# Sliding-window attention with an MLP behind it: a third buffer for natural keys and queries, fillers in each cycle of the opening, and the later mask built in the middle

## The chip, the core and the metric

The kernel runs on one core of one Trainium2 chip. The core has five engines that run side by side and wait for each other through semaphores: TensorE (matmul, PE in the profile), VectorE (DVE), ScalarE (ACT), GpSimd (POOL) and SyncE (SP). SyncE and GpSimd issue the transfers between the main memory and the on-chip memory (SBUF); matmuls write into a small accumulator memory (PSUM). Each engine takes its instructions strictly in the order in which the program gives them. The metric is the device time of the whole program in microseconds (us); lower is better. The profile also shows the clock that TensorE was granted, as a share of its full speed.

## The reference

There are 8 batches of 8 heads over 576 positions with 64 elements per head. Each position sees the positions at most 32 away, and 8 global positions see and are seen by all. The result is reordered to 4608 tokens of 512 features and goes through an MLP with a 2048 wide hidden layer and the activation `h * cos(h)`.

```python
mask = np.abs(pos[:, None] - pos[None, :]) <= 32
mask = mask | is_global[:, None] | is_global[None, :]
scores = np.where(mask, scale * np.matmul(q, k.transpose(0, 1, 3, 2)), -1e9)
attn = softmax(scores)
x = np.matmul(attn, v).transpose(0, 2, 1, 3).reshape(4608, 512)
h = x @ w_in
out = (h * np.cos(h)) @ w_out
```

## The kernel before, in words

**Units of work.** Two heads form a pair; there are 32 pairs, four to a batch, and two pairs (four heads) form a half, numbered s. For a pair the program forms scores in blocks of keys (`scores`, L673), takes the exponential on ScalarE, multiplies with a 0/1 mask on VectorE (this gives `pm`), multiplies with the values into the accumulator `pv` (`values`, L694), scales by the reciprocal of the sums (`xn`, VectorE), and turns the result into `xT` (`turn_x`, L718), which is the MLP's input with features on partitions.

**Two ways of loading.** The first four halves (pairs 0 to 7, `HY` = 4) take their keys and queries in natural order: `load_qk` (L271) lets GpSimd's queue bring the keys and the queries of a half, cast to fp16, into `kn` and `qn`, of which there are two buffers each, used in turn. `local_k` and `local_q` (L580, L591) turn them on TensorE, and ScalarE copies them out; pairs 0 to 3 also pick their global rows there (`pick_globals`). Their values come in fp32 through SyncE's queue (`load_vn`, five transfers, L368; `load_vn_rows`, the global rows, two transfers, L376) and are cast by GpSimd (`cast_vn`, L388). These pairs use five blocks and the mask `mask5` (`scores5`, `values5`, `turn_x5`). All later pairs use eleven blocks and the mask `mask` and come through casts into fp16 copies in the main memory (`cast_half`, L259, GpSimd's queue) and transposing transfers from there (`turn_half`, L278, SyncE's queue). The global rows of k, q and v are fetched by `gather` (L328, indirect transfers on GpSimd's queue).

**Later mask.** `build_mask` (L411) forms `mask` on VectorE in two parts. The first part needs two index tables that GpSimd writes (L955, L956); the second part ends with L437, L439 and L441.

**Order.** The schedule is written by hand. Behind some setup, the list `FRONT` (L57) orders the opening, in which pairs 0 to 7 run; each word is a step: `s`, `p` and `x` with a pair's number are its scores, its values and the turn of its result; `k` and `q` its local keys and queries; `L` loads keys and queries of a half, `W` a quarter of w_in (`load_w_in`), `O` w_out; `C` casts a half's values; `Y` runs `late_iotas` (a gather and the two index tables); `Z0` and `Z1` are the two parts of the later mask, `Z2` clears; `H0` casts the gathered rows and `H1` turns them; `g` copies the global columns of a pair; `c` and `K` cast the v and the k and q of a half into the main memory; `B` starts the turns and value loads of a half; `m` is one group of first-layer matmuls and `t` its activation; `+` and `-` allow or forbid the use of spare accumulators. `f` with a number issues so many fillers (`fill`, L471): matmuls of ones, 128 by 128 weights and 184 columns, into a part of `pv` that nothing reads. `MID` (L49) orders the work of s = 3, where `1` is a first-layer group with its activation and `2` a part of a second-layer sum; then follow the lists for the other halves, and at the end the rest of the MLP alone.

**w_out.** Its fp16 tile `w_out16` is allocated beside `w_in16`, is filled by step `O`, and is first read at s = 4.

Of the kernel before, what the change touches and what calls it, by code (L numbers as in the profile page):

```python
# [10 lines left out]
FP16 = mybir.dt.float16  # L11
# [6 lines left out]
B, H, S, D = 8, 8, 576, 64  # L18
NT, DM, DFF = 4608, 512, 2048
P = 128  # L20
NP = H // 2
QB = 56
NB = 11
G = 8
# [21 lines left out]

ORDER = "sa 2 2 2 2 sz pa 1 1 2 xa pz G 1 1 2 xz n 1 1 2 kc qc 1 kd qd 2 1"

MID = "+ 1 1 1 1 Z1 K5 1 1 1 1 A0 n0 Z2 1 1 A1 1 1 kc qc n1 1 1 kd qd V K6 1 1 A2 n2 - B5 1 1"  # L49

FOURTH = ORDER

# [1 line left out]

SIXTH = "sa 2 2 2 2 sz pa 1 1 2 xa pz G 1 1 2 xz n 1 1 D0 2 kc qc D1 1 kd qd D2 2 1"

FRONT = ("s0 k1 q1 L2 Y0 w4 y0 s1 p0 k2 q2 Z0 f4 x0 p1 s2 W0 C1 H0 k3 q3 L3 f4 x1 H1 p2 s3 g4 g5 k4 q4 W1 C2 x2 p3 "  # L57
         "s4 g6 g7 k5 q5 x3 C3 c4 K4 p4 s5 k6 q6 W2 x4 p5 s6 k7 q7 W3 O x5 p6 s7 B4 m m x6 p7 t t + m m t t x7 -")
WARM = 13
OK_ALL = float(P * (B * NP * 2 * BP + B))  # L60

# [143 lines left out]
def kernel(  # L205
# [41 lines left out]
    xT = keep.tile([P, NC, NT + 40], FP16)  # L247

    NV = 4
    kT = [keep.tile([P, 2, KT], FP16, name=f"kT{i}") for i in range(2)]  # L250
    qT = [keep.tile([P, 2, QT], FP16, name=f"qT{i}") for i in range(2)]
    kn = [keep.tile([KP, 2 * 2, RW, D], FP16, name=f"kn{i}") for i in range(2)]
    qn = [keep.tile([QP, 2 * 2, RW, D], FP16, name=f"qn{i}") for i in range(2)]
    vw = [keep.tile([P, NB, 2, D + 1], FP16, name=f"vw{i}") for i in range(NV)]
    NK = 4
    kw = [keep.tile([P, NB, P], FP16, name=f"kw{i}") for i in range(NK)]
# [14 lines left out]
    def load_qk(s, hs=(0, 4)):  # L271

        base = (s * 4 + hs[0]) * S * D
        for src, dst in ((k, kn[s % 2][KPAD : KPAD + S // RW]), (q, qn[s % 2][0 : S // RW])):
            nc.gpsimd.dma_start(dst[:, hs[0] : hs[1]].rearrange("x h r d -> x h (r d)"),
                                dview(src, base, (RW * D, S // RW), (S * D, hs[1] - hs[0]), (1, RW * D)))

# [25 lines left out]
    def pick_globals(pr, t, src, ones, n, to):  # L303

        h0 = 2 * (pr % 2)
        for r in range(RW):
            for h in range(2):
                nc.tensor.matmul(t[h * D : (h + 1) * D], src[:n, h0 + h, r], ones[:n, r], start=r == 0, stop=r == RW - 1, skip_group_check=True)
        nc.scalar.copy(to, view(t, (0, to.shape[1]), (1, G)))
# [18 lines left out]
    def gather(src, dst, half):  # L328
        rows = src.rearrange("b h s d -> (b h s) d")
        for h in range(2):  # L330
            nc.gpsimd.indirect_dma_start(
                out=dst[:, half, h], out_offset=None, in_=rows,
                in_offset=bass.IndirectOffsetOnAxis(ap=gidx_rows[:, 0:1], axis=0),
                element_offset=(half * 32 + h) * S * D)
# [46 lines left out]
    def hold(pr):  # L381

        nc.gpsimd.tensor_copy(gate, qb[pr % NK][0:1, 0, G : G + 1])
# [155 lines left out]


    w_in16 = const.tile([P, NC, DFF], FP16)
    w_out16 = const.tile([P, NF, DM], FP16)

    r_all = keep.tile([P, B * NP, 2 * BP], FP32)
    x_sq = keep.tile([P, B * NP // 2], FP32)
# [24 lines left out]
    def turned(src, pr, n):  # L570

        bank = ps.tile([P, 512], FP32, tag="h", bufs=2, name="bank")
        t = view(bank.bitcast(FP16), (QP, RW), (1, QP))
        h0 = 2 * (pr % 2)
        for r in range(RW):
            for h in range(2):
                nc.tensor.transpose(t[h * D : (h + 1) * D, r, 0:n], src[:n, h0 + h, r], ident16[:n, :n])
        return t, bank[:, 400 : 400 + G]

    def local_k(pr):  # L580
        to = kw[pr % NK][:, :, G:]
        if pr < 2 * HY:
            t, g = turned(kn[pr // 2 % 2], pr, KP)
            if pr < HY:
                pick_globals(pr, g, kn[pr // 2 % 2], one_k, KP, k5(pr)[:, :, 0:G])
            nc.scalar.copy(k5(pr)[:, :, G:].rearrange("p n (j r) -> p n j r", r=RW),
                           view(t, (KS // RW, NK5), (1, KS // RW), (QP, RW)))
        else:
            nc.vector.tensor_copy(to, view(kT[pr // 2 % 2][:, pr % 2], (QB, NB), (1, W)))  # L589

    def local_q(pr):  # L591
        to = qb[pr % NK][:, :, G:]
        if pr < 2 * HY:
            t, g = turned(qn[pr // 2 % 2], pr, QP)
            if pr < HY:
                pick_globals(pr, g, qn[pr // 2 % 2], one_q, QP, q5(pr)[:, 1:, 0:G])
            nc.scalar.copy(qb[pr % NK][:, 0, 0:G], t[:, :, 0])
            nc.scalar.copy(q5(pr)[:, :, G:].rearrange("p n (j r) -> p n j r", r=RW),
                           view(t[:, :, 1:], (KS // RW, NK5), (1, KS // RW), (QP, RW)))
        else:  # L600
            nc.vector.tensor_copy(to, view(qT[pr // 2 % 2][:, pr % 2], (QB, NB), (1, QB)))
# [21 lines left out]
    def values5(pr):  # L623
        pm, vp, h0 = pm_of.pop(pr), vn16(pr // 2), 2 * (pr % 2)
        X = D + 1

        def add(h, t, c0, m, slot, p0, start, stop):
            nc.tensor.matmul(pv[p0 : p0 + m, h, X * slot : X * slot + X], pm[:, h * CN + OFF[t] + c0 : h * CN + OFF[t] + c0 + m], vp[:, t, h0 + h],  # L628
                             start=start, stop=stop, skip_group_check=True)

        for group in ((0, 1, 4), (2, 3)):
            for t in group:
                for h in range(2):
                    add(h, t, D if t else 0, P if t < 4 else WID[4] - D, t, 0, t == 0, False)
            for t in group:
                for h in range(2):
                    if t:
                        add(h, t, 0, D, t - 1, D, False, t == 3)
                    else:
                        add(h, 0, P, G, 1, 0, False, False)  # L640
        den = pv[:, :, D : D + 1]
        rp = r_all[:, pr]
        dg = work.tile([G, 2], FP32, tag="dg")
        nc.vector.tensor_reduce(dg, view(pv[0:G, :, X + D : X + D + 1], (512, 2), (X, 4)), AX.X, ALU.add)
        nc.vector.reciprocal(view(rp, (NK5, 2), (1, NK5)), view(den, (512, 2), (X, NK5)))
        nc.vector.reciprocal(view(rp[0:G, 1:], (NK5, 2), (1, 4)), view(dg, (1, 2), (0, 4)))
        if pr % 2 == 0:
            xn_of[pr // 2] = work.tile([P, 2, BP, P], FP16, tag="xn", bufs=4, name="xn")
        xn = xn_of[pr // 2][:, pr % 2]
        nc.vector.tensor_tensor(  # L650
            view(xn, (D, 2), (P, NK5), (1, D)), view(pv, (512, 2), (X, NK5), (1, D)),
            view(rp, (NK5, 2), (1, NK5), (0, D)), ALU.mult)
# [209 lines left out]
    with tc.manual_schedule():  # L862
# [2 lines left out]
        nc.vector.memset(ones16, 1.0)  # L865
        nc.vector.memset(pio2, pi / 2.0)
        nc.vector.memset(kn[0][0:KPAD, 0:2], 0.0)
        for t in (qn[0][64:QP, 2:4], kn[0][0:KPAD, 2:4], qn[1][64:QP], kn[1][0:KPAD]):
            nc.scalar.memzero(t.rearrange("p a b c -> p (a b c)"))
        load_qk(0, (0, 2))  # L870
        nc.gpsimd.iota(p_i, pattern=[[0, 1]], base=0, channel_multiplier=1)
# [12 lines left out]
        build_band()  # L884
        index_rows(1)
        load_vn(0)
        gather(v, vg32, 0)
        load_qk(1)
        build_ones()
        build_mask5()  # L890
        local_k(0)
# [2 lines left out]
        warm(4)  # L894
        for s in range(1, HY):
            nc.vector.memset(vn_of(s)[0 : 64 if s == 1 else 32, 0], 0.0)
        for s in range(1, HY):
            load_vn(s)
            load_vn_rows(s)
        for i in range(NV):  # L900
            nc.vector.memset(vw[i][:, :, :, D : D + 1], 1.0)
            if i % 2:
                nc.vector.memset(vw[i][:, NB - 1, :, 0:D], 0.0)
        cast_vn(0)
        gather(k, kg32, 0)
        pv = ps.tile([P, 2, 512], FP32, tag="pv", bufs=1)
        nc.vector.memset(pv, 0.0)
        nc.vector.memset(view(pv[:, :, D : D + 1], (512, 2), (65, 6)), 1.0)
# [40 lines left out]
            load_values(2 * s)  # L949
            load_values(2 * s + 1)  # L950

        def late_iotas(_):

            gather(q, qg32, 0)
            nc.gpsimd.iota(kid_i, pattern=[[QB, NB]], base=-(G + 32), channel_multiplier=1)  # L955
            nc.gpsimd.iota(d_i, pattern=[[-1, C]], base=0, channel_multiplier=1)  # L956

        LOCAL = {"k": local_k, "q": local_q}
        OTHER = LOCAL | {"g": globals_kq, "L": load_qk, "W": load_w_in, "c": lambda s: cast_half(s, "v"), "v": load_values, "n": x_squares,
                 "C": cast_vn, "w": warm, "y": value_rows, "Y": late_iotas, "V": lambda _: hold(9), "H": early_globals, "Z": steady_buffers, "f": fill, "r": load_vn, "A": later_rows, "D": later_globals, "O": load_w_out, "K": lambda s: cast_half(s, "kq" if s == 4 else "vkq"), "B": bring, "m": lambda _: one(False), "t": lambda _: mlp_act()}  # L960
        ready[0] = 1
        for step in FRONT.split():
            if step in "+-":
# [89 lines left out]
```

## Time and profile before

| what | value |
|---|---|
| time, median of 3 runs | 367.63 us (366.43 to 369.79) |
| the profiled execution's own time | 364.79 us |
| its span, first to last instruction | 362.9 us |
| mean granted clock of TensorE | 0.949 |
| TensorE, matmuls busy | 339.1 us (93%) |
| VectorE busy | 253.4 us (70%) |
| ScalarE busy | 239.3 us (66%) |
| GpSimd busy | 107.3 us (30%) |
| moved by DMA | 45.69 MB, mean 126 GB/s |

The times of the rows of a timeline are the start, in us from the span's beginning, and the length; then come the engine, the line of the program, the operation, the tiles written and read, their shapes, and how many; in brackets stands how long the engine stood before it and what let it go. `q0` is the DMA queue that GpSimd fills, `q1` the one that SyncE fills. A row by stretches has its bounds and its length, then busy time and instructions of an engine, and behind them the granted clock, the DMA engines' busy share and GB/s.

### The profile page before, as it was taken

Reading aid. Unit: us, or ns where it says so; the run is one execution under the profiler, and the core shown is the slowest. Engines: PE = TensorE matmul, PEld = TensorE weight load, DVE = VectorE, ACT = ScalarE, POOL = GpSimd, SP = SyncE. Lnnn points to the kernel's source line nnn. Section 1 sums busy time; section 2 is a strip of 40 time slices with the busy share of each in tenths; the row PEclk is TensorE's granted clock in tenths of the full one; section 3 lists DMA queues with packets and bytes.
Section 4 is the critical chain, followed back from the end, with each engine's and each line's share of the span. In section 5 each row is a group of like instructions: output and inputs, shape, how many; then the busy total and the mean of one; then the engine's idle time right before and its main releaser. Section 6 shows DMA issues by size and latency. Waiting matters only on the chain.

```text
span 362.9 us, 8183 instructions
## 1 busy us (share of the span) xinstructions
PE 339.1 (93%) x3076; PEld 172.0 (47%) x3076; DVE 253.4 (70%) x600; ACT 239.3 (66%) x408; POOL 107.3 (30%) x218
## 2 busy tenths in 40 slices
PE   7787999688989899999999999999999999999992
PEld 3566764244444444445444445454444444444440
DVE  6758769877798768787877879686878355446310
ACT  6744686595767686868777787777877855644300
POOL 6567544652516404250605070402002000000000
PEclk9956559899999999999999999999999999999998
DMA  5999599999999999999999999999910001100111
GB/s 91 185 168 185 86 140 176 200 166 136 154 198 148 203 184 137 188 131 206 120 200 116 186 129 174 134 178 161 105 49 12 31 29 48 41 29 30 60 58 66
DMA packets 175559, 45.69 MB, mean 126 GB/s; under 512 B 163881, under 2 KB 170521, under 8 KB 175321
## 3 DMA queue, kind: packets, MB, share of 16 engines
q1 hardware_dynamic: 111657, 27.53, 54.1%
q0 software_dynamic: 63856, 17.57, 49.8%
q8 instruction: 26, 0.43, 0.5%
q14 instruction: 20, 0.16, 0.2%
HBM read 45.07 MB, written 20.05 MB: 179 GB/s over the span
## 4 chain that ended last, share of the span: by engine, by line
PE 75%; DVE 7%; DMA 6%; ACT 5%; issue 3%; SPq 3%; POOL 0%; ACTq 0%
PE po L763 32%; PE ph L746 30%; PE tx L728 2%; PE pv L628 2%; PE st L683 2%; DMA vn<-in_v_dram 2%; PE pv L703 2%; ACT e L686 2%; DMA vw<-vg 2%; DMA gidx_col<-in_global_idx_dram 1%; ACT e L691 1%; ACT cos L752 1%; PE pn L795 1%; DVE g L753 1%; SPq L402 1%
## 5 line engine op out<-in xcount | busy, mean ns | idle before, releaser
L746 PE MATMUL ph<-xT,w_in 128*128 128x512 f16 x576 | 144.3, 385 | 4.1 <-DVE g L753 2.9
L752 ACT ACTIVATE cos<-ph,pio 128x512 f16<-128x512 f32 x144 | 97.3, 687 | 68.9 <-PE ph L746 64.5
L763 PE MATMUL po<-w_out,g 128*128 128x512 f16 x576 | 139.4, 379 | 0.2 <-ACT o L768 0.2
L753 DVE TENSOR_TENSOR g<-cos,ph 128x512 f16<-128x512 f16 x144 | 96.1, 685 | 48.6 <-ACT cos L752 47.1
L746 PEld LDWEIGHTS <-w_in 128*128 128x128 f16 x576 | 54.6, 99 | 70.1 <-issue 12.7
L763 PEld LDWEIGHTS <-g 128*128 128x128 f16 x576 | 55.3, 98 | 65.5 <-issue 0.2
L937 POOL COPY gate<-xn 1x1 f16<-1x1 f16 x12 | 2.2, 181 | 132.3 <-DVE xn L714 132.3
L686 ACT ACTIVATE e<-st 128x512 f16<-128x512 f32 x48 | 26.0, 594 | 11.8 <-PE st L683 9.1
L687 DVE TENSOR_TENSOR pm<-e,mask 128x512 f16<-128x512 f16 x48 | 20.4, 426 | 19.1 <-ACT e L686 17.7
L268 POOL DMA_DIRECT2D q<-in_q_dram x12 | 26.1, 2175 | 0.0
L714 DVE TENSOR_TENSOR xn<-pv,r_all 128x768 f16<-128x768 f32 x24 | 23.0, 958 | 1.1
L781 ACT ACTIVATE xn<-xn 128x1536 f16<-128x1536 f16 (+1 forms) x16 | 22.8, 1422 | 0.0
L768 ACT COPY o<-po 128x512 f32<-128x512 f32 x18 | 10.6, 586 | 16.3 <-PE po L763 16.3
L268 POOL DMA_DIRECT2D k<-in_k_dram x12 | 19.8, 1652 | 0.2 <-issue 0.2
L770 DVE COPY o<-po 128x512 f32<-128x512 f32 x18 | 12.4, 690 | 8.8 <-PE po L763 8.2
L736 POOL COPY xT<-xg 128x4 f16 x48 | 15.4, 321 | 5.5 <-DVE xT L731 2.9
L616 ACT ACTIVATE e<-st 128x488 f16<-128x488 f32 x16 | 8.3, 572 | 13.0 <-PE st L613 13.0
L752 ACT ACT_TABLE_LOAD x13 | 16.7, 1283 | 0.2
L589 DVE COPY kw<-kT 128x1320 f16<-128x1320 f16 x24 | 16.3, 679 | 0.0
L628 PE MATMUL pv<-vw,pm 128*128 128x65 f16 (+3 forms) x160 | 13.4, 230 | 2.4 <-issue 1.1
L686 ACT ACT_TABLE_LOAD x12 | 15.4, 1283 | 0.2
L703 PE MATMUL pv<-vw,pm 128*64 128x65 f16 x528 | 14.0, 197 | 1.7 <-DMA vw<-vg 1.2
(173 smaller groups left out, 365.1 us busy)
## 6 DMA issues: line engine op xcount, KB each, us to landing
out_dram<-o SPq DMA_DIRECT2D x36, 256.0 KB
vw<-v SPq DMA_DIRECT2D x35, 165.0 KB
v<-in_v_dram POOLq DMA_DIRECT2D x12, 288.0 KB, 5.6
k<-in_k_dram POOLq DMA_DIRECT2D x12, 288.0 KB, 8.0
q<-in_q_dram POOLq DMA_DIRECT2D x12, 288.0 KB, 9.4
w_in<-in_moe_w_in_dram POOLq DMA_DIRECT2D x4, 512.0 KB
w_out<-in_moe_w_out_dram POOLq DMA_DIRECT2D x1, 2048.0 KB
vn<-in_v_dram SPq DMA_DIRECT2D x16, 120.0 KB
```

Of the source, the lines that this page charges most:

```text
L268: nc.gpsimd.dma_start(dst[s].rearrange("t (h d) -> t h d", h=4), dview(src, base, (D, S), (S * D, 4), (1, D)))
L589: nc.vector.tensor_copy(to, view(kT[pr // 2 % 2][:, pr % 2], (QB, NB), (1, W)))
L628: nc.tensor.matmul(pv[p0 : p0 + m, h, X * slot : X * slot + X], pm[:, h * CN + OFF[t] + c0 : h * CN + OFF[t] + c0 + m], vp[:, t, h0 + h], ...
L686: nc.scalar.activation(e[:, 0:512], st[h], AF.Exp, scale=scale)
L687: nc.vector.tensor_tensor(view(pm[:, h], (1, 512)), e[:, 0:512], view(mask, (1, 512)), ALU.mult)
L703: nc.tensor.matmul(pv[r0 : r0 + C, j // 6, c0 : c0 + 65], pm[:, h, j], vp[:, j, h], start=True, stop=True)
L714: nc.vector.tensor_tensor(view(xn, (384, 2), (D, 6), (1, D)), view(pv, (512, 2), (65, 6), (1, D)), view(rp, (6, 2), (1, 6), (0, D)), ALU.mult)
L746: nc.tensor.matmul(ph, w_in16[:, j, f * P : (f + 1) * P], xT[:, j, t * TT : (t + 1) * TT], start=(j == 0), stop=(j == NC - 1))
L752: nc.scalar.activation(cos, ph, AF.Sin, bias=pio2)
L753: nc.vector.tensor_tensor(g, cos, ph, ALU.mult)
L763: nc.tensor.matmul(po, g16[:, f, s * P : (s + 1) * P], w_out16[:, f], start=(f == 0), stop=(f == NF - 1))
L781: nc.scalar.activation(view(xn, (BP * P, 2), (1, n)), view(xn, (BP * P, 2), (1, n)), AF.Square, accum_out=x_sq[:, s : s + 1])
```

## The change

- `kn` and `qn` get a third buffer each, which lies in the room of `w_out16`; that tile is now allocated earlier. `load_qk` of half 2 is issued right behind that of half 1, and that of half 3 where half 2's stood. ScalarE clears the unused rows of the third buffers too.
- The two index tables are written before the first gather. The gather of k moves from the setup into step `Y`, where it stands together with that of q, behind the load of half 3.
- The values of half 2 are loaded before the global rows of half 1, and those of half 3 before the rows of half 2.
- `Z0` moves from `FRONT` to `MID`, where it stands right before `Z1`.
- `FRONT` has eight fillers before p0 and six before each of x0 to x5; before, it had four before x0 and four before x1. The steps `C`, `W`, `H`, `g` and `O` are placed anew.
- In `values5` all matmuls on whole blocks come first and those on the neighbours' parts behind them; before, blocks 0, 1 and 4 had both ahead of blocks 2 and 3.
- In `MID` one step `1` moves ahead of `A2`, and the spare accumulators are forbidden one place later.

```diff
-MID = "+ 1 1 1 1 Z1 K5 1 1 1 1 A0 n0 Z2 1 1 A1 1 1 kc qc n1 1 1 kd qd V K6 1 1 A2 n2 - B5 1 1"
+MID = "+ 1 1 1 1 Z0 Z1 K5 1 1 1 1 A0 n0 Z2 1 1 A1 1 1 kc qc n1 1 1 kd qd V K6 1 1 1 A2 n2 B5 - 1"
...
-FRONT = ("s0 k1 q1 L2 Y0 w4 y0 s1 p0 k2 q2 Z0 f4 x0 p1 s2 W0 C1 H0 k3 q3 L3 f4 x1 H1 p2 s3 g4 g5 k4 q4 W1 C2 x2 p3 "
-         "s4 g6 g7 k5 q5 x3 C3 c4 K4 p4 s5 k6 q6 W2 x4 p5 s6 k7 q7 W3 O x5 p6 s7 B4 m m x6 p7 t t + m m t t x7 -")
+FRONT = ("s0 k1 q1 L3 Y0 w4 y0 s1 f8 p0 k2 q2 f6 x0 p1 s2 C1 W0 k3 q3 f6 x1 p2 s3 H0 k4 q4 f6 x2 H1 g4 g5 C2 p3 "
+         "s4 W1 k5 q5 f6 x3 g6 g7 p4 s5 k6 q6 C3 c4 K4 f6 x4 p5 s6 k7 q7 W2 W3 O f6 x5 p6 s7 B4 m m x6 p7 t t + m m t t x7 -")
...
+    NN = 3
...
+    w_out16 = const.tile([P, NF, DM], FP16)
+    kn.append(w_out16[0:KP, 0:4].rearrange("p h (r d) -> p h r d", d=D))
+    qn.append(w_out16[0:QP, 4:8].rearrange("p h (r d) -> p h r d", d=D))
...
-        for src, dst in ((k, kn[s % 2][KPAD : KPAD + S // RW]), (q, qn[s % 2][0 : S // RW])):
+        for src, dst in ((k, kn[s % NN][KPAD : KPAD + S // RW]), (q, qn[s % NN][0 : S // RW])):
...
-        for group in ((0, 1, 4), (2, 3)):
-            for t in group:
-                for h in range(2):
-                    add(h, t, D if t else 0, P if t < 4 else WID[4] - D, t, 0, t == 0, False)
-            for t in group:
-                for h in range(2):
-                    if t:
-                        add(h, t, 0, D, t - 1, D, False, t == 3)
-                    else:
-                        add(h, 0, P, G, 1, 0, False, False)
+        for t in (0, 1, 4, 2, 3):
+            for h in range(2):
+                add(h, t, D if t else 0, P if t < 4 else WID[4] - D, t, 0, t == 0, False)
+        for t in (1, 4, 2, 3):
+            for h in range(2):
+                add(h, t, 0, D, t - 1, D, False, False)
+        for h in range(2):
+            add(h, 0, P, G, 1, 0, False, True)
...
-        for t in (qn[0][64:QP, 2:4], kn[0][0:KPAD, 2:4], qn[1][64:QP], kn[1][0:KPAD]):
+        for t in (qn[0][64:QP, 2:4], kn[0][0:KPAD, 2:4], qn[1][64:QP], kn[1][0:KPAD], qn[2][64:QP], kn[2][0:KPAD]):
...
         load_vn(0)
+        nc.gpsimd.iota(kid_i, pattern=[[QB, NB]], base=-(G + 32), channel_multiplier=1)
+        nc.gpsimd.iota(d_i, pattern=[[-1, C]], base=0, channel_multiplier=1)
         gather(v, vg32, 0)
         load_qk(1)
+        load_qk(2)
...
-        for s in range(1, HY):
-            load_vn(s)
-            load_vn_rows(s)
+        load_vn(1)
+        load_vn(2)
+        load_vn_rows(1)
+        load_vn(3)
+        load_vn_rows(2)
+        load_vn_rows(3)
...
         cast_vn(0)
-        gather(k, kg32, 0)
...
-        def late_iotas(_):
+        def late_gathers(_):
 
+            gather(k, kg32, 0)
             gather(q, qg32, 0)
-            nc.gpsimd.iota(kid_i, pattern=[[QB, NB]], base=-(G + 32), channel_multiplier=1)
-            nc.gpsimd.iota(d_i, pattern=[[-1, C]], base=0, channel_multiplier=1)
```

More of the change, by code (lines that the diff above doesn't have):

```diff
@@ L541 @@
     w_in16 = const.tile([P, NC, DFF], FP16)
-    w_out16 = const.tile([P, NF, DM], FP16)
     r_all = keep.tile([P, B * NP, 2 * BP], FP32)
@@ L582, in local_k @@
         if pr < 2 * HY:
-            t, g = turned(kn[pr // 2 % 2], pr, KP)
+            t, g = turned(kn[pr // 2 % NN], pr, KP)
             if pr < HY:
-                pick_globals(pr, g, kn[pr // 2 % 2], one_k, KP, k5(pr)[:, :, 0:G])
+                pick_globals(pr, g, kn[pr // 2 % NN], one_k, KP, k5(pr)[:, :, 0:G])
             nc.scalar.copy(k5(pr)[:, :, G:].rearrange("p n (j r) -> p n j r", r=RW),
@@ L593, in local_q @@
         if pr < 2 * HY:
-            t, g = turned(qn[pr // 2 % 2], pr, QP)
+            t, g = turned(qn[pr // 2 % NN], pr, QP)
             if pr < HY:
-                pick_globals(pr, g, qn[pr // 2 % 2], one_q, QP, q5(pr)[:, 1:, 0:G])
+                pick_globals(pr, g, qn[pr // 2 % NN], one_q, QP, q5(pr)[:, 1:, 0:G])
             nc.scalar.copy(qb[pr % NK][:, 0, 0:G], t[:, :, 0])
@@ L950, in bring @@
             load_values(2 * s + 1)
-        def late_iotas(_):
+        def late_gathers(_):
+            gather(k, kg32, 0)
             gather(q, qg32, 0)
-            nc.gpsimd.iota(kid_i, pattern=[[QB, NB]], base=-(G + 32), channel_multiplier=1)
-            nc.gpsimd.iota(d_i, pattern=[[-1, C]], base=0, channel_multiplier=1)
         LOCAL = {"k": local_k, "q": local_q}
         OTHER = LOCAL | {"g": globals_kq, "L": load_qk, "W": load_w_in, "c": lambda s: cast_half(s, "v"), "v": load_values, "n": x_squares,
-                 "C": cast_vn, "w": warm, "y": value_rows, "Y": late_iotas, "V": lambda _: hold(9), "H": early_globals, "Z": steady_buffers, "f": fill, "r": load_vn, "A": later_rows, "D": later_globals, "O": load_w_out, "K": lambda s: cast_half(s, "kq" if s == 4 else "vkq"), "B": bring, "m": lambda _: one(False), "t": lambda _: mlp_act()}
+                 "C": cast_vn, "w": warm, "y": value_rows, "Y": late_gathers, "V": lambda _: hold(9), "H": early_globals, "Z": steady_buffers, "f": fill, "r": load_vn, "A": later_rows, "D": later_globals, "O": load_w_out, "K": lambda s: cast_half(s, "kq" if s == 4 else "vkq"), "B": bring, "m": lambda _: one(False), "t": lambda _: mlp_act()}
         ready[0] = 1
```

## The prediction

> **What bounds the kernel now.** First the head of the page, then the busy time by stretches of 3.41 us, the step in which the granted clock changes here.
>
> ```profile
> span 362.9 us, 8183 instructions
> PEclk9956559899999999999999999999999999999998
> ```
>
> ```profile
> 25.59:29.00 3.41, 1.93 (x59) 0.50 1.31 180
> 29.00:32.41 3.41, 3.41 (x40) 0.50 1.16 198
> 32.41:35.83 3.42, 2.63 (x63) 1.00 1.16 171
> 35.83:39.24 3.41, 3.41 (x61) 0.50 0.96 160
> 52.89:56.30 3.41, 3.41 (x35) 1.00 1.22 197
> ```
>
> ```profile
> 160.00:280.00 120.00, 119.47 (x1150) 58.65 (x1148) 96.61 (x218) 91.41 (x148) 29.39 (x72) 1.00 1.30 137
> ```
>
> In the first fence a slice is a fortieth of the span. In the second the columns are the stretch, its length, TensorE's busy time and instructions, and its granted clock. The slice row shows the clock at half in slices 4 to 6. The stretches show that being busy isn't enough: at 35.83 TensorE is busy throughout at clock 0.50, while 32.41 ran at 1.00 with 2.63 us busy. The last row shows the steady part: TensorE busy 119.47 of 120 us at full clock. So what the change can win or lose lies before it, in the eight pairs of the opening and in the middle (MID), and a microsecond there reaches the end nearly whole. The profiled execution took 364.79 us, 1.9 more than its span; the median shown, 367.63, is 2.8 above it. I sum against 364.79 and put the difference on 367.63.
>
> The opening is read from the timelines of TensorE and VectorE. I call the start of the value matmuls (L628) of pair n "p n".
>
> ```profile
> 23.53 0.94 DVE L415 CAST kid<-kid_i 128x11 f32<-128x11 int32 x1 [4.11 <-POOL kid_i L955]
> 26.63 0.47 DVE L663 COPY xT<-tx 128x600 f16<-128x600 f16 x1
> 29.90 1.84 PE L628 MATMUL pv<-vw,pm 128*128 128x65 f16 x20
> 35.82 0.91 PE L613 MATMUL st<-qb,kw 64*128 64x136 f16 x10
> 38.32 1.85 PE L628 MATMUL pv<-vw,pm 128*128 128x65 f16 x20
> 40.10 0.91 PE L613 MATMUL st<-qb,kw 64*128 64x136 f16 x10
> 53.49 1.25 PE L628 MATMUL pv<-vw,pm 128*128 128x65 f16 x20
> 54.68 1.90 PE L746 MATMUL ph<-xT,w_in 128*128 128x512 f16 x8
> ```
>
> VectorE stood 4.11 us at the first half of the later mask, waiting for GpSimd's iota, and needed 3.1 us for it (23.53 to 26.63). That held up p 2, at 29.90. From there p 4 came at 38.32 and p 7 at 53.49. A cycle at half clock, scores to scores, is 40.10 - 35.82 = 4.28 us, all TensorE.
>
> **The change part by part.**
>
> *Mask and iotas out of the opening.* This removes the 4.11 + 3.1 = 7.2 us. The iotas go into GpSimd's wait before its first gather (next fence, 1.21 us) and cost nothing. What is late next is the data of p 2.
>
> *Loads sooner.* The two DMAs of the third k and q load move from 19.14, where GpSimd came out of 2.71 us of register reads, to about 11 us; the fourth load takes the place at 16 to 19 us. On the queue that GpSimd fills (q0), the gathers of k and q now stand behind both; on SyncE's (q1), the global rows of the second half pair stand behind all of the third half pair's values.
>
> ```profile
> 6.87 1.08 POOL L331 DMA_INDIRECT vg<-in_v_dram,gidx_rows  x1 [1.21 <-DVE one_k L301]
> 19.14 0.78 POOL L275 DMA_DIRECT2D kn<-in_k_dram  x1 [2.71 <-issue]
> 24.35 1.31 POOL L390 CAST vw<-vn 128x1280 f16<-128x1280 f32 x1
> ```
>
> ```profile
> vn<-in_v_dram SPq DMA_DIRECT2D x16, 120.0 KB
> kn<-in_k_dram POOLq DMA_DIRECT2D x3, 288.0 KB
> vn<-in_v_dram SPq DMA_DIRECT2D x4, 96.0 KB
> vn<-vg SPq DMA_DIRECT2D x6, 20.0 KB
> ```
>
> The next three fences are the DMA view from 0 to 17 us, from 22 to 26 and from 26 to 28: packets, MB moved, and share of the engines.
>
> ```profile
> q0 software_dynamic: 1691, 1.25, 51.9%
> q1 hardware_dynamic: 4275, 1.00, 33.4%
> ```
>
> ```profile
> q0 software_dynamic: 635, 0.52, 84.8%
> q1 hardware_dynamic: 658, 0.18, 27.9%
> ```
>
> ```profile
> q1 hardware_dynamic: 917, 0.23, 100.9%
> q0 software_dynamic: 104, 0.10, 30.2%
> ```
>
> No stall on a k or q load of pairs 4 to 7 stands in the timelines, so the earlier load by itself removes none. Its price is on q1. Values of one half pair are (16 x 120 + 4 x 96) / 4 = 576 KB, or 0.59 MB. Before the cast of the second (C1 on GpSimd, 1.31 us) may start, q1 must now have moved three of these and 0.04 MB of rows, 1.81 MB; at 17 us it has moved 1.00, so 0.81 are left. At 17 us q0 has just moved two k and q loads (0.59 each, a k of 288 KB and a q like it) and the first gather, 1.25. In the new order it has 1.18 of loads ahead. While q0 moves such loads it gets 0.13 MB a us and q1 only 0.045 (22 to 26): q0 is done at 26.1, and q1 has moved 0.41. Then come the gathers, 0.13 MB at 0.05 a us (26 to 28), to 28.7, with 0.30 more on q1. The last 0.1 at the 0.115 a us of that row takes 0.9 us: 29.6. C1 ends at 30.9, and p 2 starts there, **1.0 us later** than at 29.90. If the queues shared 0.175 evenly, q1 would be through at 26.3 and p 2 at 27.7, 2.2 sooner; if gathers also starve q1, about 32, 2 later. I take the row of 22 to 26, as it has the same two loads on the same queues. Behind C1 on GpSimd wait the first w_in load and the casts of the gathered rows, whose data come at 28.7, earlier; behind p 2 on TensorE wait all later pairs.
>
> *Fillers.* Six matmuls of 184 columns before each turn of x, eight before p 0. At half clock four took 0.77 us, so six take 1.15; at full clock half of that.
>
> ```profile
> 28.59 0.77 PE pv L475 x4
> ```
>
> ```profile
> 16.64 1.16 PE L628 MATMUL pv<-vw,pm 128*128 128x65 f16 x17 [1.15 <-issue]
> 35.92 0.15 DVE L644 TENSOR_REDUCE dg<-pv 8x2 f32<-8x8 f32 x1 [0.31 <-PE pv L628]
> 37.20 0.73 DVE L617 TENSOR_TENSOR pm<-e,qT 128x488 f16<-128x488 f16 x2
> 38.28 0.56 DVE L621 TENSOR_TENSOR pm<-e,qT 128x768 f16<-128x768 f16 x1 [0.35 <-ACT e L620]
> 41.49 1.78 DVE L617 TENSOR_TENSOR pm<-e,qT 128x488 f16<-128x488 f16 x2
> ```
>
> The eight lie in the 1.15 us for which TensorE stood before p 0. The others sit between p n and p n+1. With p 2 late, TensorE idles before it as from 25.59 to 29.00, and the clock stays at half until a filled stretch has passed, say 35.8: p 2 to p 3 is 4.28 + 1.15 + 0.2 for the turned globals = 5.6 us. Then at full clock the bound is VectorE's chain: from dg (35.92) to the end of the last mask product (38.84) 2.92 us. In the *new order of the value matmuls* six are ready before that product and 14 of 20 come after it, 0.88 us of the 1.25 that p 7 took at full clock; in the old order it was eight, 0.50. A cycle is 2.92 + 0.88 = 3.8 us, 0.38 of it by the new order; fillers and the turn hide beside the mask products. p 2 to p 4: 5.6 + 3.8 = 9.4 against 8.4, **1.0 us later**. p 4 to p 7: two of 3.8; one with eight MLP matmuls in it, 1.25 + 0.46 (half of 0.91) + 1.90 + 0.3 for the turn = 3.9; and 1.0 for the cast that holds VectorE's product (1.78 against 0.73): 12.5 against 15.2, **2.7 us sooner**, which is the clock's gain. Together the opening is 0.7 us shorter.
>
> *The mask in the middle.* Before, the second half alone stood there.
>
> ```profile
> 61.78 0.30 DVE L432 TENSOR_TENSOR eq<-kid,gf 128x88 f32<-128x88 f32 x1
> 63.31 2.45 DVE L439 TENSOR_SCALAR mask<-val,own 128x88 f16<-128x88 f32 x1
> 66.74 10.46 PE L746 MATMUL ph<-xT,w_in 128*128 128x512 f16 x40 [2.87 <-DVE g L753]
> ```
>
> ```profile
> 63.55 2.19 POOL L268 DMA_DIRECT2D q<-in_q_dram  x1
> 73.29 0.53 DVE L589 COPY kw<-kT 128x1320 f16<-128x1320 f16 x1
> ```
>
> L439 stood until GpSimd had issued the q cast (63.55 + 2.19 = 65.74); then L441 let go at 66.1, and TensorE had waited 2.87 us. Now the first half comes ahead. At its own 3.1 us it ends at 64.9, the four operations of the second before L439 take 1.53 more (61.78 to 63.31), and L439, no longer held, and L441 0.6: 67.0, **0.9 us later**. Least is nothing, if the first half runs free in the time in which L439 was held anyway; most is 2.65, if its first tensor_scalar is held to 65.74 with 3.0 us of work behind it. I take 0.9, from its own row. The Trainium skill's page "SBUF — State Buffer" (section "SBUF: two separate sides") says that VectorE in a two-port mode and GpSimd exclude each other and the loser waits for the whole instruction; L439 agrees (2.45 us), and by that rule the 2.65 would be likelier, the sum 1.8 us worse.
>
> *Rest.* Two more clears on ScalarE run before its first copy; they add to a stretch in which it has idle time, no cost taken. The casts of the fifth half pair start 1 to 2 us later, behind x 3; their reader is L589 at 73.29, far behind. w_out's load waits for matmuls of pair 5, long done.
>
> **Sum:** + 1.0 + 1.0 - 2.7 + 0.9 = + 0.2. So 365.0 for such an execution, 367.8 as a median: no change that can be told.
>
> **Rivals.** *Loads come evenly and the clock holds.* p 2 at 27.7 (- 2.2), both cycles to p 4 at 3.8 (- 0.8), p 4 to p 7 in 11.5 (- 3.7), the middle free: - 6.7, **360.9**. For it: the 7.2 us of the mask do leave the path. Against it: 0.045 MB a us on q1. Chance 0.30.
>
> *The fillers don't hold the clock.* The slower one, placed between p 2 and p 7. Stretches at full clock were lost with 2.63 us busy (32.41, next at 0.50); a new cycle has 1.25 of values and 0.58 of fillers in 3.8 us. If that falls short, TensorE is the bound again, at 4.28 + 1.15 = 5.4 a cycle: p 2 to p 4 11.0 (+ 2.6), p 4 to p 7 two of 5.4 and one of 1.85 + 0.91 + 2 x 1.90 = 6.6 (+ 2.2). With + 1.0 and + 0.9: + 6.7, **374.3**. It decides once over half of the stretches from 36 us on are at 0.50. The Trainium skill's page "TensorE: Matmul & The Clock Gate" (section "PE-mode transpose") says that transposes do not count as busy for the gate; that would take the turns of k, q and x out of the account and speaks for this rival. Its rule of thumb (same page, "Why this matters for your kernels") that only idle gaps of about 3 us lose the clock speaks against it, but the stretch at 32.41 lost it with no such gap. Chance 0.27.
>
> *The earlier loads do nothing and hurt nothing*, p 2 as before and the rest as summed: - 0.8, 366.8; this lies inside the forecast.
>
> **Numbers.** The forecast, with the last rival, has 0.40, the fast case 0.30, the slow one 0.27; 0.03 is left for other things. Within 1% (3.7 us) is about what a measurement can tell from no change. From the fast case a little lands within 1%, from the forecast little lies beyond: faster 0.31, same 0.39, slower 0.30. The range cuts into both outer cases: 361.5 to 373.5; the forecast's own is 364.6 (the loads at their early end) to 370.6 (loads and middle at their late ends).
>
> **What would show it.** C1's end and p 2 near 30.9, with q1 moving 0.05 MB a us from 17 to 26; the clock at 1.00 from about 36 to 53 and p to p of 3.8; VectorE's mask work in the middle over 5 us and TensorE's wait there near 3.8; the steady part unchanged. Wrong: p 2 before 28, or a clock at half after 40, or q1 not starved.

## The result, and the profile after

The changed kernel takes 369.97 us in the median of 20 runs (369.11 to 371.38), the kernel before 366.99 us in 20 runs beside them (365.24 to 369.79). The ratio is 1.0075, with a 95% interval of 1.0056 to 1.0095: slower by about 2.8 us, inside the 1% that I had set as "no change that can be told", though the interval leaves out 1. The predicted time was 367.8 us. The profiled execution of the changed kernel took 369.96 us, as its median; that of the kernel before took 364.79 us, 2.2 under its median, and this turns out to matter. A line of the code has a number one to four higher than before (L628 is L631 now, L746 is L747, L264 is L268).

The head of the page of the changed kernel:

```profile
span 368.3 us, 8258 instructions
PEclk9985899899899999999999999999999999999999
```

The clock is at half in slice 4 only, where before it was low in slices 3 to 6 (the prediction read that row as 4 to 6). By stretches of 3.41 us (stretch, length, TensorE's busy time and instructions, clock, share of the DMA engines, GB/s) the changed kernel shows:

```profile
28.99:32.41 3.42, 0.17 (x2) 0.50 0.81 135
35.82:39.23 3.41, 3.41 (x55) 0.50 0.87 146
39.23:42.64 3.41, 3.01 (x71) 0.98 0.02 5
46.06:49.47 3.41, 2.83 (x70) 1.00 0.39 53
```

TensorE stood nearly all of 29 to 32.4 us, then ran at half clock to about 39, then at full clock. Four of its value matmuls, p 2, p 4, p 6 and p 7, in the timeline of TensorE:

```profile
33.41 1.54 PE L631 MATMUL pv<-vw,pm 128*128 128x65 f16 x20 [4.25 <-POOL vw L394]
42.09 0.38 PE L631 MATMUL pv<-vw,pm 128*128 128x65 f16 x6
49.47 0.38 PE L631 MATMUL pv<-vw,pm 128*128 128x65 f16 x6
53.32 1.21 PE L631 MATMUL pv<-vw,pm 128*128 128x65 f16 x20
```

So p 2 is 3.5 us later than before (29.90), p 4 3.8 later, and p 7 0.2 *sooner* (53.49 before). The opening as a whole costs nothing here. Nor does the middle. Three rows of VectorE's timeline (the mask operation that GpSimd's issue holds, and the first copies of turned keys and queries of pair 8), then three of TensorE's (its wait in the middle and two later ones):

```profile
64.37 1.17 DVE L443 TENSOR_SCALAR mask<-val,own 128x88 f16<-128x88 f32 x1
73.19 0.53 DVE L592 COPY kw<-kT 128x1320 f16<-128x1320 f16 x1
77.31 0.47 DVE L604 COPY qb<-qT 128x616 f16<-128x616 f16 x1 [3.59 <-DMA qT<-q]
```

```profile
66.53 8.75 PE L747 MATMUL ph<-xT,w_in 128*128 128x512 f16 x32 [2.88 <-DVE g L754]
78.43 1.89 PE L747 MATMUL ph<-xT,w_in 128*128 128x512 f16 x8 [3.15 <-DVE g L754]
93.31 0.81 PE L704 MATMUL pv<-vw,pm 128*64 128x65 f16 x22 [2.39 <-DMA vw<-vg]
```

TensorE's wait in the middle is 2.88 us against 2.87 before. At 73.19 VectorE copies the turned keys of pair 8, 0.1 us sooner than before (73.29). Up to here the two traces are level. The next two rows are where the time goes: VectorE waits 3.59 us for the turned *queries* of pair 8, and TensorE stands 3.15 us behind it; at 93.31 TensorE waits for value rows. TensorE's busy time by stretches shows the same, first of the kernel before and then of the changed one:

```profile
56.00:75.00 19.00, 16.13 (x72) 0.91 1.34 182
75.00:100.00 25.00, 23.14 (x210) 1.00 1.69 153
```

```profile
56.00:75.00 19.00, 16.12 (x71) 0.91 1.26 200
75.00:100.00 25.00, 17.70 (x157) 0.93 1.67 155
160.00:280.00 120.00, 119.46 (x1153) 1.00 1.34 145
```

From 75 to 100 us TensorE works 5.4 us less. The steady part is what it was (119.47 then, 119.46 now). The chain that ended last, of the changed kernel, names what stands ahead of p 2 and of the value matmuls at 93 us (start, length, what; SPq is SyncE's queue of DMA issues):

```profile
23.78 1.39 SPq L380
...
25.22 6.64 DMA vn<-vg
...
32.10 1.26 POOL vw L394
```

```profile
74.79 4.22 SPq L406
...
84.06 2.76 SPq L406
...
86.87 6.69 DMA vw<-vg
```

### The profile page after: what moved, and what is told of

It is laid out like the page before. It is cut to its first block, busy times and chain, and to the rows that moved or that the text cites. A ratio compares the mean times of both kernels' runs of the same rounds, so it can differ in the third digit from the quotient of the medians.

```text
span 368.3 us, 8258 instructions
## 1 busy us (share of the span) xinstructions
PE 336.0 (91%) x3112; PEld 170.4 (46%) x3112; DVE 248.0 (67%) x600; ACT 241.4 (66%) x410; POOL 106.6 (29%) x218
## 4 chain that ended last, share of the span: by engine, by line
PE 74%; SPq 7%; ACT 5%; DMA 5%; DVE 4%; issue 3%; POOL 0%; ACTq 0%; POOLq 0%
PE po L764 32%; PE ph L747 31%; SPq L372 4%; PE tx L729 3%; PE st L684 2%; SPq L406 2%; DMA vw<-vg 2%; ACT e L687 2%; DMA vn<-vg 2%; PE pv L631 2%; PE pv L704 2%; DMA gidx_col<-in_global_idx_dram 1%; ACT e L692 1%; PE pn L796 1%; SPq L354 1%
## 5 line engine op out<-in xcount | busy, mean ns | idle before, releaser
L747 PE MATMUL ph<-xT,w_in 128*128 128x512 f16 x576 | 144.9, 386 | 7.8 <-DVE g L754 6.0
L747 PEld LDWEIGHTS <-w_in 128*128 128x128 f16 x576 | 54.7, 99 | 73.4 <-issue 15.7
L272 POOL DMA_DIRECT2D k<-in_k_dram x12 | 19.8, 1652 | 0.2 <-issue 0.2
L631 PE MATMUL pv<-vw,pm 128*128 128x65 f16 (+3 forms) x160 | 9.8, 207 | 5.5 <-POOL vw L394 4.3
```

Source lines behind the costliest of these rows:

```text
L272: nc.gpsimd.dma_start(dst[s].rearrange("t (h d) -> t h d", h=4), dview(src, base, (D, S), (S * D, 4), (1, D)))
L747: nc.tensor.matmul(ph, w_in16[:, j, f * P : (f + 1) * P], xT[:, j, t * TT : (t + 1) * TT], start=(j == 0), stop=(j == NC - 1))
```

## The experiments

**The theory.** A half pair is a half of the description above, two pairs; half pair 1 is the second of them, and the fifth is half 4. In the new order SyncE issues the global rows of half pair 1 only behind the values of half pair 2, so C1, the cast of half pair 1's values on GpSimd, ends late. Everything behind C1 on GpSimd moves with it, also the casts of the fifth half pair (c4 and K4: its v, k and q from DRAM). From those casts hangs a chain on SyncE's queue, the turns of k and q and then all the value copies of the later pairs. By the first profile it came in time in the kernel before; now it is late, and TensorE waits at 75 to 100 us. Rivals: the waits there have another cause (the early load, the mask in the middle); or the loss is the fillers' own.

In the timeline of GpSimd the casts start at 47.75 in the changed kernel:

```profile
32.10 1.25 POOL L394 CAST vw<-vn 128x1280 f16<-128x1280 f32 x1 [6.62 <-DMA vn<-vg]
47.75 0.55 POOL L268 DMA_DIRECT2D v<-in_v_dram  x1
```

In the kernel before it was

```profile
42.95 0.55 POOL L264 DMA_DIRECT2D v<-in_v_dram  x1
```

so they are 4.8 us later. Each of the next four kernels changes one thing in the changed kernel.

**rows_first**: the rows ask for the queue as they did before.

```
-        load_vn(2)
         load_vn_rows(1)
-        load_vn(3)
+        load_vn(2)
         load_vn_rows(2)
+        load_vn(3)
```

> The changed kernel with one edit undone: each half's global rows of the values are again asked for right behind that half's values (values 1, rows 1, values 2, rows 2, values 3, rows 3). Theory A (the rows of half 1 stand on SyncE's queue behind the values of half 2, so the cast C1 is late, p 2 is late, and with them GpSimd's later steps up to the casts of half 4): C1 starts near 25.5 us instead of 32.1, p 2 near 29 instead of 33.4, the casts of half 4 start near 43.5 instead of 47.75, and the waits between 75 and 100 us (3.15 and 2.39 us) shrink to under 1.5 together; total 364 to 366, 4 to 6 below the changed kernel. Rival B (it is the early load of keys and queries that starves that queue, whatever the order of the rows): C1 stays at 30 or later, and the total within 1.5 of the changed kernel's 370. Rival C (the later waits have another cause): p 2 sooner, but the total stays near 370.

Measured: 364.12 us, ratio to the kernel before 0.9891 (0.9823 to 0.9959), so 1.8% under the changed kernel. C1 starts at 25.48 instead of 32.10, p 2 at 27.55, p 7 at 47.84, and the casts at 42.26. The order of two lines alone is worth more than all that the change lost. But p 7 came 5.5 us sooner, and TensorE still waits behind it, for value rows, 1.44 us at 79.7 and 4.45 us at 87.7, where I had expected under 1.5 us in all:

```profile
87.73 1.03 PE L704 MATMUL pv<-vw,pm 128*64 128x65 f16 x22 [4.45 <-DMA vw<-vg]
```

The chain says what stands ahead of it:

```profile
41.12 1.20 POOL vw L394
42.81 6.35 DMA k<-in_k_dram
49.18 2.31 SPq L284
51.59 6.89 SPq L285
58.65 11.31 DMA vw<-v
...
77.98 9.71 DMA vw<-vg
```

From the end of C3 (L394) at 42.3 to the landing of the first values at 70.0 no step of it is on a compute engine: the cast of k, its turn, the turn of q and the value copy, one behind the other, the last three on SyncE's queue. The value rows at 78 to 87.7 hang on the same queue.

**load2_late**: the third k and q load at its old place, the fourth behind k3 q3.

```
-FRONT = "s0 k1 q1 L3 Y0 ... W0 k3 q3 f6 x1 ..."
+FRONT = "s0 k1 q1 L2 Y0 ... W0 k3 q3 L3 f6 x1 ..."
...
         load_qk(1)
-        load_qk(2)
```

> The changed kernel with the loads of keys and queries asked for where they were before (half 2 behind q1, half 3 behind k3 and q3; three buffers stay). Theory A: the values' queue is less contended from 17 to 19 us, but the rows of half 1 still stand behind the values of half 2: C1 starts at 26 to 30, p 2 at 29 to 31; total 366 to 369. Rival B: C1 starts before 26, p 2 at 29 or sooner, total under 366. If the early load does no harm at all, C1 stays at 32 and the total at 370.

Measured: 365.10 us, ratio 0.9946 (0.9913 to 0.9979), 0.9 us under the least that I had expected. C1 starts at 27.30, the casts at 42.95. SyncE issued the ten value loads ahead of the rows in 9.32 us here and in 14.14 us in the changed kernel. The early load and the order of the rows share the blame for C1; undoing either one brings most of it back.

**casts_early**: c4 and K4 go from behind C3 to behind H0; C1 stays late.

```
-FRONT = ("... p2 s3 H0 k4 q4 f6 x2 ... C3 c4 K4 f6 x4 p5 ...")
+FRONT = ("... p2 s3 H0 c4 K4 k4 q4 f6 x2 ... C3 f6 x4 p5 ...")
```

> The changed kernel with the casts of half 4 (c4, K4) issued right behind H0 on GpSimd, before the copies for pair 4, instead of behind C3; nothing else moves. Theory A: the opening stays as it is (p 2 at 33.4, p 7 at 53 to 54), the casts start near 35 instead of 47.75, the wait for the turned queries of half 4 (3.15 us at 75) is gone and the wait for the values' rows of pair 9 (2.39 at 91) shrinks: total 364.5 to 367. Rival C (the waits between 75 and 100 us have another cause, as w_out or the order of the middle): these waits stay, total 369 to 371.

Measured: 361.36 us, ratio 0.9822 (0.9758 to 0.9886): 2.5% (about 9 us) under the changed kernel, and 1.8% under the kernel before, 3.1 us better than the best that I had expected. The opening is nearly as late as in the changed kernel (p 2 at 32.70, p 7 at 52.40), and the waits are gone:

```profile
75.00:100.00 25.00, 23.83 (x239) 1.00 1.76 161
```

That settles the rival about the waits: with early load, late rows, moved mask and fillers all in place, the casts' start alone removes them. On GpSimd the moved casts also pass C2, C3 and a load of w_in; what that adds isn't separated.

**no_fillers_in_cycles**: the six f6 are gone, f8 stays.

> The changed kernel without the six fillers before each of x0 to x5; the eight before p 0 stay. If the fillers hold the clock: granted clock 0.5 in most of 36 to 52 us instead of 1.0, a cycle 4.3 us instead of 3.7, p 7 some 2 us later than 53.3, total 371 to 373. If the clock doesn't hang on them: clock 1.0 from 40 to 53, cycles 3.6, total 369 to 370.

Measured: 370.26 us, ratio 1.0052 (1.0016 to 1.0088), not to be told from the changed kernel. The clock rose at 40 us without them, and stayed up with TensorE busy for even less of a stretch:

```profile
35.82:39.23 3.41, 3.41 (x57) 0.50 0.69 118
39.23:42.64 3.41, 2.86 (x67) 0.85 0.25 20
42.64:46.06 3.42, 2.60 (x65) 1.00 0.84 138
```

So the fillers weren't what kept the clock up in the changed kernel, which I had expected.

**rows_and_casts**: both repairs, with the casts behind C2.

```
-FRONT = ("... H1 g4 g5 C2 p3 " "... C3 c4 K4 f6 x4 p5 ...")
+FRONT = ("... H1 g4 g5 C2 c4 K4 p3 " "... C3 f6 x4 p5 ...")
```

and the lines of rows_first.

> The changed kernel with both repairs: the rows of half pair 1 ask for SyncE's queue ahead of the values of half pair 2, and the casts of the fifth half pair are issued by GpSimd behind C2. Theory A (the two delays add: p 2 late by the queue, the stretch 75 to 100 us late by the casts): p 7 near 48 as in rows_first, no waits for turned queries or values behind it as in casts_early, so 361.4 less the 4 to 5 us of the opening: 357. Rival (the work behind the opening has another floor, such as the values gathered and loaded for later pairs, that an earlier opening only uncovers): TensorE's waits at 75 to 100 us come back, 360 to 362.

Measured: 361.44 us, ratio 0.9799 (0.9738 to 0.9860). The opening is 3.2 us shorter than that of casts_early (p 7 at 49.20 against 52.40), and the time is the same. The rival of this run was right: another floor takes over. In its profiled execution (364.29 us) TensorE waits for value rows of later pairs, longest at 84.39:

```profile
84.39 0.22 PE L704 MATMUL pv<-vw,pm 128*64 128x65 f16 x2 [1.99 <-DMA vw<-vg]
```

**rows_casts_old_value_order**, **rows_casts_no_fillers**, **rows_casts_plain**: rows_and_casts with the value matmuls in the order of the kernel before, without the six fillers, and with both.

> The kernel of rows_and_casts with the value matmuls in the order of the kernel before. If the new order costs 0.38 us in each full-clock cycle, as the prediction has it, the cycles go from 3.7 to 3.3 and five of them win 1.5 to 2 us. If the new order is what lets TensorE reach its full clock at 36 to 40 us, the clock goes back to one half there and the time rises by 3 to 5 us. If it is neither, within 0.5 us of rows_and_casts.

> The kernel of rows_and_casts without the six fillers of each cycle (the eight ahead of p 0 stay). As in no_fillers_in_cycles: the clock reaches 1.00 without them, and the time is within 0.7 us of rows_and_casts. If the fillers matter only while the data of p 2 come early, the clock stays at 0.50 past 40 us and the time rises by 3 us or more.

> The kernel of rows_and_casts without the six fillers and with the value matmuls in the old order: what is left of the change is the loads, the mask and the eight fillers ahead of p 0. If neither fillers nor value order matter, within 1 us of rows_and_casts and rows_casts_no_fillers, 359.5 to 361.5. If one of them makes up for the other, 3 us or more above.

Measured: 362.25 us (ratio 0.9818, 0.9754 to 0.9883), 359.85 us (0.9782, 0.9722 to 0.9842) and 360.48 us (0.9824, 0.9768 to 0.9879). None of the three can be told from rows_and_casts. With the old value order a full-clock cycle, p 3 to p 4 and p 4 to p 5, is 3.55 and 3.69 us; with the new one 3.47 and 3.64. The 0.38 us that I charged for the new order don't show in these cycles. Without the six fillers (the second of the three) the clock here did stay at half, past 46 us:

```profile
35.82:39.23 3.41, 3.41 (x61) 0.50 1.19 111
39.23:42.64 3.41, 3.41 (x50) 0.50 2.16 163
```

and a cycle was 4.2 us. Of the two answers in the expectation the clock went the second way and the time the first: p 7 is at 49.68 against 49.20, since rows_and_casts loses in one cycle most of what it won in the others (p 5 to p 6 takes 5.55 us, with 1.34 us in which TensorE waits for GpSimd's L569, queued behind the casts' issues and eight copies of L672 that took 3.51 us).

**before_casts_early**: the kernel before, with c4 and K4 behind C2.

```
-FRONT = ("... W1 C2 x2 p3 " "... C3 c4 K4 p4 ...")
+FRONT = ("... W1 C2 c4 K4 x2 p3 " "... C3 p4 ...")
```

> The kernel before with one edit: the casts of the fifth half pair issued by GpSimd behind C2 instead of behind C3. Theory A says that in the kernel before they were in time (TensorE idles only 1.9 us in 75 to 100 us), so at most 1 to 1.5 us are to be had: 366 to 367.5. If early casts are worth as much there as in the changed kernel (8.6 us), their lateness isn't what the change brought: 359 to 361.

Measured: 363.79 us, ratio 0.9874 (0.9816 to 0.9931), 4.8 us under the runs of the kernel before beside it. That is neither answer. The casts were *not* in time in the kernel before, though its first profile shows hardly a wait. With the casts early in both, the changed kernel is no slower than the kernel before (casts_early 0.9822, here 0.9874, with intervals that overlap): what the change lost goes with the casts. The next run asks whether the first profile was the usual one.

**before_second_profile**: the kernel before, unchanged, profiled again.

> The kernel before, unchanged, for a second profile: the first was of a quick execution (364.79 us, 2.2 below the median of 20 runs). If casts that are barely in time are what spreads its executions, the second shows more idle time of TensorE at 75 to 130 us (4.5 us or more of 55 us, where the first had 4.5) with waits for turned queries or value rows, and the same opening (p 2 near 29.9 to 30.8, p 7 near 53.5 to 55). If the spread comes from the opening, p 7 is 2 us or more later than 53.5 and the stretch 75 to 130 us is as in the first.

This execution took 366.59 us, near the median. Its casts start at 44.34 instead of 42.95, p 7 is at 54.23, and TensorE's work in 75 to 100 us and its longest wait there are

```profile
75.00:100.00 25.00, 20.43 (x171) 0.93 1.70 157
```

```profile
89.36 0.22 PE L703 MATMUL pv<-vw,pm 128*64 128x65 f16 x2 [3.28 <-DMA vw<-vg]
```

So an execution near the median waits for late value rows too; the first profile showed one in which they came just in time. Set against this execution, the changed kernel works 2.7 us less from 75 to 100 us (17.70), close to the 2.8 us by which it is slower.

**mask_only**: the kernel before with iotas and mask moved, nothing else.

```
-FRONT = "... p0 k2 q2 Z0 f4 x0 ..."
+FRONT = "... p0 k2 q2 f4 x0 ..."
-MID = "+ 1 1 1 1 Z1 K5 ..."
+MID = "+ 1 1 1 1 Z0 Z1 K5 ..."
...
         load_vn(0)
+        nc.gpsimd.iota(kid_i, ...)
+        nc.gpsimd.iota(d_i, ...)
```

> The kernel before with the mask part alone: iotas ahead of GpSimd's first gather, the first half of the mask in the middle. By the prediction VectorE's 7.2 us go off the path of p 2, and C1 (its end near 25.7) or the turned globals are what is late next: p 2 at 27 instead of 29.9, the middle 0 to 0.9 later, so 1 to 3 us under the kernel before, 364.5 to 366.5. Theory A adds that the casts of the fifth half pair start about as much earlier as p 2 does, which may give 1 to 2 more. Rival (VectorE's mask was covered by something else that holds p 2): p 2 within 0.5 of 29.9 and the time unchanged.

Measured: 367.66 us, ratio 0.9988 (0.9952 to 1.0025): nothing. The rival was right about the time. p 2 is at 30.61, as in the second profile of the kernel before (30.77), where I had expected 27. With VectorE free, TensorE stood before p 2 for something else, the global queries, which GpSimd casts:

```profile
30.18 0.29 POOL L514 CAST g<-qg 128x128 f16<-128x128 f32 x1 [3.98 <-DMA qg<-in_q_dram,gidx_rows]
```

```profile
30.53 0.29 PE L536 MATMUL t<-ident,g 128*128 128x128 f16 x1 [3.98 <-POOL g L514]
30.61 0.58 PE L628 MATMUL pv<-vw,pm 128*128 128x65 f16 x6
```

The mask's 7.2 us lay beside a gather that landed at nearly the same time. In the kernel before, the same cast came at 28.94:

```profile
28.94 0.39 POOL L514 CAST g<-qg 128x128 f16<-128x128 f32 x1 [3.04 <-DMA qg<-in_q_dram,gidx_rows]
```

**mask_and_casts**: mask_only with the casts behind C2.

> The kernel of mask_only with the casts of the fifth half pair behind C2. If the gain of the mask part and of the early casts (4.8 us in before_casts_early) add, 360 to 362. If the early casts take all that there is behind the opening, and later values are the floor, 362.5 to 364, the time of before_casts_early.

Measured: 364.32 us (three of the four runs 362.49 to 364.85), ratio 0.9898 (0.9824 to 0.9972), not to be told from before_casts_early. No gain of the mask shows.

All profiled executions, one of each kernel and two of the kernel before, in order of the casts' start (timeline of GpSimd), with p 7:

| kernel | casts start | p 7 | execution, us |
|---|---|---|---|
| changed | 47.75 | 53.32 | 369.96 |
| no_fillers_in_cycles | 46.78 | 52.36 | 370.78 |
| mask_only | 44.45 | 54.60 | 367.88 |
| before, second profile | 44.34 | 54.23 | 366.59 |
| before, first profile | 42.95 | 53.49 | 364.79 |
| load2_late | 42.95 | 48.52 | 365.22 |
| rows_first | 42.26 | 47.84 | 365.29 |
| rows_and_casts | 35.00 | 49.20 | 364.29 |
| before_casts_early | 34.86 | 55.23 | 363.90 |
| rows_casts_old_value_order | 34.85 | 48.90 | 363.00 |
| rows_casts_plain | 34.23 | 49.75 | 360.45 |
| casts_early | 34.10 | 52.40 | 359.39 |
| mask_and_casts | 34.07 | 53.47 | 363.80 |
| rows_casts_no_fillers | 33.90 | 49.68 | 359.73 |

From 42 us on the time follows the casts, about 1 us for each and within some 1 us (5.5 us from 42.26 to 47.75, 4.7 us of time), and not p 7: rows_first has p 7 5.65 us ahead of the first profile of before and takes 0.5 us longer. Up to 35 us neither the casts nor p 7 order the executions (359.4 us with p 7 at 52.40, 364.3 with 49.20). What sets the time there isn't shown.

The lowest median of these, that of rows_casts_no_fillers with 359.85 us, is 2.2% under the kernel before (0.9782, 0.9722 to 0.9842); the other kernels with both repairs and casts_early can't be told from it.

## Why the prediction was right, and where it was wrong

The time lay well inside the range and within 1% as forecast; the reason was another. The opening and the middle were forecast to cancel, and they did, by luck: p 2 was missed by + 2.5 us, and the other three terms by - 0.7, - 1.2 and - 0.9. What made the kernel 2.8 us slower is a step that I had costed at nothing. Of the signs that I had named, the clock (0.98 and more from 39.2 us) and the cycles came true; C1's end (33.35), q1's rate, the mask's 4.3 us in the middle and TensorE's 2.88 us there did not.

- **C1 and p 2, + 1.0: sign right, size wrong.** It measured + 3.5. The DMA view of the changed kernel from 17 to 26 us (packets, MB, share of the engines):

```profile
q0 software_dynamic: 1363, 0.99, 72.4%
q1 hardware_dynamic: 2615, 0.65, 53.6%
```

  q1 moved 0.65 MB in 9 us, 0.072 MB a us where I had 0.045, and by 28.2 us it had moved 1.80 MB (values of the fourth half pair among them), sooner than the 29.6 that I had for 1.81; by volume alone C1 would have been ready sooner than I said. I had treated the queue as bytes in a row. The rows weren't *issued* before 23.78, as SyncE took 14.1 us to issue the ten value loads ahead of them, and then needed 6.64 us to land (the chain above). In the timeline of SyncE the ten loads are

```profile
9.53 14.14 SPq L372 DMA_DIRECT2D vn<-in_v_dram  x10
```

  The Trainium skill's page "DMA: Bandwidth & Descriptors" (section "Queues, rings and completion order") says that the engines serve the queues in turn by packets. From 22 to 26 us, the next fence, the packets are nearer to even than the bytes, but from 17 to 26 us they are 1363 against 2615, so the trace doesn't settle it. Why the rows took 6.6 us isn't shown by a run.

```profile
q0 software_dynamic: 690, 0.51, 87.8%
q1 hardware_dynamic: 843, 0.21, 38.8%
```

- **"That held up p 2"** (of the mask) was true by little at most. In the kernel before, the global queries were cast by 29.33 (the row shown with mask_only), 0.6 us ahead of p 2, and mask_only, which takes the mask out, left p 2 no sooner (30.61). The 7.2 us weren't there to be won by the mask alone.
- **p 2 to p 4, + 1.0; p 4 to p 7, - 2.7.** Measured: 8.68 us against 8.42, + 0.3, and 11.23 against 15.17, - 3.9. The clock was late to rise (39 instead of 35.8), and still the terms were better than forecast: three cycles of 3.69, 3.69 and 3.85, near the 3.8 and 3.9, but no microsecond for the cast beside VectorE's product. The sum of the opening is - 0.2, forecast - 0.7.
- **The new value order, 0.38 a cycle.** No run shows this cost; the cycles of rows_casts_old_value_order are no shorter.
- **The middle, + 0.9.** Measured 0, the lower bound. Before, L439 was held until GpSimd's issue ended; now the first half runs free while GpSimd issues, and L443 is held for 1.17 instead of 2.45 us. The Trainium skill's page "SBUF — State Buffer" (section "SBUF: two separate sides"), by which the 2.65 would have been likelier, fits L443, which was held to the end of that issue (65.52). The operations ahead of it ran beside the same issues and weren't held; whether they are of the mode that the page means isn't shown. The added work fell into time that was lost before as well.
- **The failed step is "Rest": "The casts of the fifth half pair start 1 to 2 us later, behind x 3; their reader is L589 at 73.29, far behind."** They started 4.8 us later, the + 3.5 of p 2 among it, and L589 isn't their only reader. The turn of q comes behind the turn of k on SyncE; in the changed kernel it was issued at 57.52 and its reader started at 77.31, 19.8 us later. In the other traces where that reader waits for it (rows_first, load2_late, no_fillers_in_cycles) this takes 18.0, 18.4 and 18.8 us. Before, it was issued at 52.65, and the reader, L601, started at 73.73 without a wait. As an estimate, with 18.0 to 19.8 us it had landed at 70.7 to 72.4 and had 1.3 to 3.1 us to spare, against 4.9 of delay; the wait that came of it is the 3.59 of the row. The value copies of the later pairs follow on the same queue, without a gap.
- **"A microsecond there reaches the end nearly whole"** was wrong as well. rows_first reaches the p 2 of the fast rival (27.55 for 27.7, by the order of the rows and not by even loads, so the match is chance) and a p 7 5.65 us sooner than the first profile of the kernel before, and is 1.1% faster than it, not the 1.8% of the rival's 6.7 us.
- **Rivals.** *The fillers don't hold the clock* didn't come true, since the clock of the changed kernel stays up; but no_fillers_in_cycles shows that it does so without them. That the mask was under cover of something else wasn't among the rivals.

The step behind all this is reading one profile of an execution 2.2 us under the median as the kernel's normal course: its TensorE wait for value rows at 75 to 100 us was nearly nothing, and I concluded that those transfers had room.

## What to carry to other kernels

When a step moves on an in-order engine, follow every DMA that it issues to *all* its readers, through the queue on which the next DMAs wait; the first reader in the listing can be the one with the most room. A wait that doesn't show in one profile isn't slack: work out the time from issue to landing and set it against the reader's start, above all where that execution is quicker than the median. And before an opening is shortened, look at what is already on the chain behind it: here moving the two steps of casts was worth 4.8 us in the kernel before, and with them moved in both the rest of the change has no effect that can be told.

## What the runs showed of the hardware

The granted clock didn't follow TensorE's busy time. It stayed at 0.50 through stretches that were busy throughout (rows_casts_no_fillers, 3.41 of 3.41 us from 35.8 to 42.6), and stayed at 1.00 in stretches that were busy for 2.60 of 3.42 us (no_fillers_in_cycles). Of the three kernels without the six fillers it rose at 40 us in no_fillers_in_cycles, and not before 46 us in rows_casts_no_fillers and rows_casts_plain. The Trainium skill's page "TensorE: Matmul & The Clock Gate" (section "PE-mode transpose") says that transposes don't count as busy in the same way, which would fit the first of these; its rule of one sustained busy window (section "What's actually happening") doesn't fit it by the busy time of the rows. What decides is open; no run takes the turns of k and q out.

A late cast showed itself 26 and 43 us after it: the 47.75 of GpSimd came out as waits of VectorE from 73.7 and of TensorE from 90.9 us, by way of SyncE's queue, which no row of busy time shows.
